# Decayed linear attention with 64 by 64 TensorE tiles, ahead of a snake feed-forward, on one core

## The chip, the core and the metric

One core of one Trainium2 chip. Its engines run their own instruction streams and meet through semaphores: TensorE (PE), VectorE (DVE), ScalarE (ACT), GpSimd (POOL), SyncE (SP), and 16 DMA engines that serve queues filled by SP and POOL. The metric is the device time of one execution in microseconds. The kernel before takes 219.55 us, the median of 5 runs (218.67 to 219.71).

## The reference

Attention with a decaying state, 4 sequences x 8 heads x 768 tokens x 64, then a feed-forward of 512 to 2048 to 512 over the 3072 tokens:

```python
gamma = 1.0 - 2.0 ** (-5.0 - np.arange(H))
for t in range(S):
    state = gamma * state + outer(k[t], v[t])        # per sequence and head
    y[t] = q[t] @ state / sqrt(D)
h = x @ w_in                                         # x: heads side by side
s = np.sin(alpha * h)
out = (h + s * s / alpha) @ w_out
```

## The kernel before

A sequence is cut in six chunks of 128 tokens, 24 chunks in all. The order P is: the four first chunks (e0 to e3), then the five others of sequence 0 (P4 to P8), of sequence 1 (P9 to P13), 2 (P14 to P18) and 3 (P19 to P23). Chunks go to the feed-forward in seven groups of 4, 2, 4, 4, 4, 4 and 2.

A chunk's attention is four steps on PE. *Scores*, `pa` (L213): per head K^T Q, 64 rows of the array by 128 columns. *Between chunks*, `py` (L247): the state times Q, with two heads' states in one block-diagonal 128 by 128 tile `s_bd`. *Mix*, `py` (L251): V times masked scores, 128 rows by 64 columns. *Sums*, `ps` (L227): K^T V added to the running state in PSUM. Each is eight matmuls, two of them side by side in the array. Around them DVE masks the scores into `aT` (L217) and scales `py` into `xT` (L258), and ACT copies `ps` to `s_bd` in two halves (L234). V is scaled by the decay beforehand (`scale_v`, L112), mostly on POOL. Q and K arrive with tokens on partitions and are turned either on PE (`stage_T`, with a copy by DVE or ACT) or by the DMA crossbar (`turn`, issued by SP, L205).

The feed-forward of a group runs in 16 slots of one 128-wide slice (8 double slots for the groups of 2): four matmuls into `ph` (L279), sine and square on ACT (L282, L287), `s * 1/alpha + ph` on DVE into `gT` (`Slot.add`, L294). Between the slots PE takes pieces of the second product of the group before (`ff_out`, `po`, L304), copied out by ACT (L316) and stored by SP.

All orders are written by hand: each engine executes what the program lists, in that order. Group 0 is interleaved by hand with the first attention chunks; `phase` runs the other groups and hangs attention steps on slots through the dictionary `att`. PSUM has eight banks: four rotate under the tag `mm` (`ph`, `po`, some `pt`), two hold `pa`, one each `ty` (`py`, `pt`) and `ps`.

POOL issues the loads, about 0.9 us for one. A load waits until the one eight before it on this queue has landed, and POOL's `scale_v` stand between the loads.

## Time and profile before

| | |
|---|---|
| median of 5 runs | 219.55 us |
| the profiled execution | 220.33 us |
| its span, first to last instruction | 218.6 us |
| PE, DVE, ACT, POOL busy | 207.2, 128.5, 162.7, 90.0 us |
| granted TensorE clock | 0.996 of full |

The profiled execution is 0.78 us over the median, and its own time is 1.8 us over its span. A row of the timeline is: start in us, length in us, engine, line, operation, output<-inputs, tile of the array, shapes, count, and in brackets how long the engine sat idle before and what ended that. Matmuls are pipelined, so lengths overlap; the distance between two starts is what a step costs.

### The profile page before, as it was taken

The page shows a single profiled execution, that of the slowest core. Times are in us where ns is not written, and L with a number is a line of the kernel's source. Part 1 is how long each engine was busy: PE and PEld are TensorE (multiplying, and loading weights), DVE is VectorE, ACT ScalarE, POOL GpSimd, SP SyncE. Part 2 cuts the span into 40 slices and gives each one's busy share as a digit, 9 for nine tenths or more (in the row PEclk, how much of TensorE's full clock was granted, in tenths as well). Part 3 has the DMA queues.
Part 4 walks back from the last instruction along what each step waited for, and adds up shares of the span by engine and source line. Part 5 has one row for each costly group of instructions (what it writes and reads, how often), then busy time and mean ns, then how long its engine had stood idle before and what let it go on. Part 6 is the DMA issues. An engine that isn't in the chain of part 4 may idle for free.

```text
span 218.6 us, 4245 instructions
## 1 busy us (share of the span) xinstructions
PE 207.2 (95%) x1661; PEld 107.4 (49%) x1661; DVE 128.5 (59%) x213; ACT 162.7 (74%) x311; POOL 90.0 (41%) x105
## 2 busy tenths in 40 slices
PE   7986899899999999999999999999999999999992
PEld 3443554457764544545455445455444544555540
DVE  4784849966896767766566556476464555233310
ACT  7776796668888999798778769768768876766610
POOL 8974434899859599293978100000000000000000
PEclk9999999999999999999999999999999999999998
DMA  9999999999999999999999946136111101111121
GB/s 132 147 190 189 206 207 165 149 192 169 163 138 176 116 154 154 113 117 165 136 183 144 78 96 76 39 82 75 25 49 51 48 0 51 48 48 48 51 93 51
DMA packets 99508, 24.67 MB, mean 113 GB/s; under 512 B 92304, under 2 KB 96416, under 8 KB 99488
## 3 DMA queue, kind: packets, MB, share of 16 engines
q0 software_dynamic: 77024, 13.37, 85.6%
q1 hardware_dynamic: 22464, 11.02, 25.9%
q8 instruction: 13, 0.21, 0.4%
q14 instruction: 7, 0.06, 0.1%
HBM read 27.27 MB, written 6.29 MB: 154 GB/s over the span
## 4 chain that ended last, share of the span: by engine, by line
PE 75%; DVE 10%; DMA 5%; POOL 4%; ACT 4%; issue 1%; POOLq 0%
PE po L304 36%; PE ph L279 31%; DMA qkr<-in_k_dram 5%; DVE gT L294 5%; PE py L247 3%; PE pa L213 2%; POOL qkr L83 2%; DVE aT L217 2%; PE py L251 2%; ACT s L282 1%; POOL vr L83 1%; DVE xT L258 1%; ACT s L287 1%; PE ps L227 1%; DVE s L289 1%
## 5 line engine op out<-in xcount | busy, mean ns | idle before, releaser
L294 DVE SCALAR_TENSOR_TENSOR gT<-s,rec_alpha,ph 128x512 bf16<-128x512 f32 (+3 forms) x120 | 74.2, 638 | 68.0 <-ACT s L287 67.4
L279 PE MATMUL ph<-xT,w_in 128*128 128x512 bf16 (+3 forms) x480 | 98.0, 337 | 1.3 <-DMA w_in<-in_moe_w_in_dram 0.5
L304 PE MATMUL po<-w_out,gT 128*128 128x512 bf16 x384 | 98.5, 380 | 0.6 <-DVE gT L294 0.6
L282 ACT ACTIVATE s<-ph,alpha_sb 128x512 f32<-128x512 f32 (+3 forms) x120 | 69.5, 601 | 35.6 <-PE ph L279 35.5
L279 PEld LDWEIGHTS <-w_in 128*128 128x128 bf16 x480 | 45.5, 98 | 42.9 <-issue 1.9
L287 ACT ACTIVATE s<-s 128x512 f32<-128x512 f32 (+1 forms) x94 | 58.4, 621 | 2.6
L304 PEld LDWEIGHTS <-gT 128*128 128x128 bf16 x384 | 35.2, 98 | 38.2 <-issue 0.6
L112 POOL TENSOR_TENSOR vr<-vr,kg 128x512 bf16<-128x512 bf16 x21 | 22.0, 1064 | 19.4 <-DMA vr<-in_v_dram 19.4
L217 DVE TENSOR_TENSOR aT<-pa,mask 128x1024 bf16<-128x1024 f32 x20 | 24.4, 1222 | 0.2 <-PE pa L213 0.2
L83 POOL DMA_DIRECT2D vr<-in_v_dram x24 | 21.8, 910 | 3.1 <-DMA w_in<-in_moe_w_in_dram 1.6
L83 POOL DMA_DIRECT2D qkr<-in_q_dram x23 | 21.3, 928 | 4.0 <-DMA w_out<-in_moe_w_out_dram 1.7
L83 POOL DMA_DIRECT2D qkr<-in_k_dram x23 | 20.6, 894 | 3.5 <-DMA w_out<-in_moe_w_out_dram 3.4
L234 ACT CAST s_bd<-ps 64x256 bf16<-64x256 f32 x40 | 14.4, 359 | 2.4 <-PE ps L227 2.1
L316 ACT COPY o_sb<-po 128x512 f32<-128x512 f32 x23 | 13.1, 575 | 4.0 <-PE po L304 3.9
L258 DVE TENSOR_TENSOR xT<-py,qg 128x512 bf16<-128x512 f32 x20 | 13.7, 685 | 2.7 <-PE py L251 2.7
L328 PE MATMUL spare<-warm 128*128 128x512 bf16 x28 | 9.5, 461 | 1.2 <-DVE warm L131 1.2
L213 PEld LDWEIGHTS <-qkT 64*128 64x128 bf16 x192 | 5.4, 94 | 9.3 <-issue 7.1
L251 PE MATMUL py<-aT,vr 128*64 128x128 bf16 x192 | 9.6, 220 | 0.4 <-DVE aT L217 0.4
L213 PE MATMUL pa<-qkT 64*128 64x128 bf16 x192 | 9.5, 219 | 0.4 <-ACT qkT L186 0.2
L247 PE MATMUL py<-qkT,s_bd 128*64 128x128 bf16 x160 | 8.3, 225 | 0.7 <-DVE xT L258 0.7
L247 PEld LDWEIGHTS <-s_bd 128*64 128x64 bf16 x160 | 5.4, 109 | 4.7 <-issue 2.0
L251 PEld LDWEIGHTS <-vr 128*64 128x64 bf16 x192 | 6.9, 110 | 1.3 <-issue 1.0
(59 smaller groups left out, 69.2 us busy)
## 6 DMA issues: line engine op xcount, KB each, us to landing
out_dram<-o_sb SPq DMA_DIRECT2D x24, 256.0 KB, 2.9
vr<-in_v_dram POOLq DMA_DIRECT2D x24, 128.0 KB, 6.5
qkr<-in_q_dram POOLq DMA_DIRECT2D x23, 128.0 KB, 5.6
qkr<-in_k_dram POOLq DMA_DIRECT2D x23, 128.0 KB, 6.0
w_in<-in_moe_w_in_dram POOLq DMA_DIRECT2D x4, 512.0 KB, 11.7
w_out<-in_moe_w_out_dram POOLq DMA_DIRECT2D x4, 512.0 KB, 15.9
q<-in_q_dram SPq DMA_DIRECT2D x1, 256.0 KB, 3.3
k<-in_k_dram SPq DMA_DIRECT2D x1, 256.0 KB, 4.1
```

Source lines behind the costliest of these rows:

```text
L83: nc.gpsimd.dma_start(out=t, in_=chunk_of(src, j))
L112: eng.tensor_mul(raw["v", j], raw["v", j], kg[:, j % NCH, :, None].to_broadcast([128, H, D]))
L213: nc.tensor.matmul(pa[:, e, p, :], qkT[r, NP + p, :], qkT[r, p, :], start=(p == 0), stop=True, skip_group_check=True)
L217: nc.vector.tensor_mul(aT.rearrange("p e n t -> p (e n) t"), pa.rearrange("p e n t -> p (e n) t"), m)
L247: nc.tensor.matmul(py[r, p, :], s_bd[c % 2][:, p, r], qkT[:, p, :], start=(p == 0), stop=True, skip_group_check=True)
L251: nc.tensor.matmul(py[64 * e:64 * e + 64, p, :], vs[:, 2 * p + e, :], aT[:, e, p, :], start=(c == 0 and p == 0), stop=True, skip_group_che ...
L258: nc.vector.tensor_mul(x, py, qg[:, c])
L279: nc.tensor.matmul(self.ph[:, m, :], w_in[:, i, f * 128:(f + 1) * 128], xT[g][:, i, self.lo:self.hi], start=(m == 0 and i == 0), stop=(i = ...
L282: nc.scalar.activation(out=self.s[:, m, :], in_=self.ph[:, m, :], func=ACTF.Sin, scale=alpha_sb[:, f:f + 1])
L287: nc.scalar.activation(out=self.s, in_=self.s, func=ACTF.Square)
L294: nc.vector.scalar_tensor_tensor(gT[self.g][:, f, self.lo:self.hi], self.s[:, m, :], rec_alpha[:, f:f + 1], self.ph[:, m, :], op0=ALU.mult ...
L304: nc.tensor.matmul(po[g, ts], gT[g][:, f, ts * C:(ts + 1) * C], w_out[:, f, :], start=(f == 0), stop=(f == FF - 1))
```

## The change

Every attention step after the first chunks takes 64 by 64 tiles where it can, four side by side: scores split each K tile in two halves of tokens (16 matmuls of 64x64 for 8 of 64x128), the step between chunks takes each head's 64 by 64 state alone (`inter`), without the block-diagonal copy. The heads' places in `xT` differ for half of the partitions, so `w_in` is loaded in three transfers instead of one. The state lives in SBUF (`s_f`, added to by DVE in `keep`) and is handed on in bf16 by one ACT copy (`hand_on`). The last sequence (`wide`) is loaded with 64 tokens per partition half, in 24 transfers (`load_seq`), its triangular halves are left out of scores and mix, its state is handed on by two POOL copies, and its `inter` is four full 128x128 matmuls. `pa` and `py` have two banks each, four are `mm`.

The steps are regrouped: a `burst` is `inter` and mix of one chunk with the scores of the next, so the mask has four slots before it is used. DVE's part of a burst is spread: mask in the slot, addition of the state and `xT` in the next; in group 1 mask and state come first, then the slot's `add`, then `xT`. P8 and P9 are turned on PE (copies on ACT), P10 and later by the crossbar, issued three chunks ahead. Later V are scaled by DVE, those of the last sequence by POOL. The last output tile leaves in three column pieces.

```diff
...
+    def wide(j):
+        return j % NCH > 0 and j // NCH == 3
+    def load_seq(bt):
+        nh = 2 * (NCH - 1)
+        tqk = big.tile([128, nh, 2, NP, D], BF16, name="qk_seq", tag="qk_seq", bufs=1)
+        tv = big.tile([128, nh, NP, D], BF16, name="v_seq", tag="v_seq", bufs=1)
+        for i, src in enumerate((q, k, v)):
+            for h in range(H):
+                r = slice(64 * (h // NP), 64 * (h // NP) + 64)
+                o = tv[r, :, h % NP, :] if i == 2 else tqk[r, :, i, h % NP, :]
+                nc.gpsimd.dma_start(out=o, in_=src[bt, h, C:, :].rearrange("(f i) d -> i f d", i=64))
+        for c in range(1, NCH):
+            j, f = bt * NCH + c, slice(2 * c - 2, 2 * c)
+            raw["qk", j], raw["k", j], raw["v", j] = tqk[:, f], tqk[:, f, 1], tv[:, f]
...
-        nc.gpsimd.dma_start(out=w_in[:, :, i * fw:(i + 1) * fw], in_=w_in_v[:, :, i * fw:(i + 1) * fw])
+        c = slice(i * fw, (i + 1) * fw)
+        nc.gpsimd.dma_start(out=w_in[:, 0:2, c], in_=w_in_v[:, 0:2, c])
+        for y in range(2):
+            nc.gpsimd.dma_start(out=w_in[64 * y:64 * y + 64, 2:4, c], in_=w_in_v[64 - 64 * y:128 - 64 * y, 2:4, c])
...
+    def later_tables():
+        for b in range(2):
+            r = slice(64 * b, 64 * b + 64)
+            for f in range(2):
+                nc.vector.tensor_scalar_add(tok[r, :, f], pos[r, :], float(64 * (f - b)))
+            nc.vector.tensor_copy(lgq[r], lg[r, NP * b:NP * b + NP])
+        for f in range(2):
+            nc.vector.tensor_mul(expoq[:, :, NP * f:NP * f + NP],
+                                 tok[:, :, f, None].to_broadcast([128, NCH, NP]),
+                                 lgq[:, None, :].to_broadcast([128, NCH, NP]))
+    def later_mask():
+        for t in s_w:
+            nc.vector.memset(t, 0.0)
+        for b in range(2):
+            nc.vector.tensor_scalar(maskq[64 * b:64 * b + 64, 0:128], tio[64 * b:64 * b + 64],
+                                    tok[64 * b:64 * b + 64, 0, 0:1], None, op0=ALU.is_ge)
...
+    s_f = big.tile([128, 2, 2, D], F32, name="s_f")
+    s_n = [big.tile([128, 2, 2, D], BF16, name=f"s_n{i}") for i in range(2)]
+    s_w = [big.tile([128, 2, 2, 128], BF16, name=f"s_w{i}") for i in range(2)]
...
+    tiles4 = [(b, e) for b in range(2) for e in range(2)]
...
+    def sums(j, py, base=256):
+        ks, vs = raw["k", j], raw["v", j]
+        for f in range(2 if wide(j) else 1):
+            for m in range(2):
+                for b, e in tiles4:
+                    o = py[half(e), b, base + 64 * m:base + 64 * m + 64]
+                    if not wide(j):
+                        h = 4 * b + 2 * m + e
+                        nc.tensor.matmul(o, ks[:, h, :], vs[:, h, :], start=(base == 0 and m == 0 and b == 0), stop=True,
+                                         skip_group_check=True)
+                    else:
+                        nc.tensor.matmul(o, ks[half(b), f, 2 * m + e, :], vs[half(b), f, 2 * m + e, :],
+                                         start=False, stop=True, skip_group_check=True)
+    def keep(j, py, base=256):
+        new = py[:, :, base:base + 128].rearrange("p b (m d) -> p m b d", m=2)
+        if j % NCH == 0:
+            nc.vector.tensor_copy(s_f, new)
+        else:
+            nc.vector.tensor_add(s_f, s_f, new)
+    def hand_on(j):
+        i = (j % NCH + 1) % 2
+        if not wide(j + 1):
+            nc.scalar.copy(s_n[i], s_f)
+            return
+        s = s_w[i].rearrange("p m b (y d) -> p m (b y) d", y=2)
+        nc.gpsimd.tensor_copy(s[half(0), :, 0:4:3], s_f[half(0)])
+        nc.gpsimd.tensor_copy(s[half(1), :, 1:3], s_f[half(1)])
+    def begin(j):
+        new = psum.tile([128, 2, 256], F32, name="new", tag="mm", bufs=4)
+        sums(j, new, 0)
+        keep(j, new, 0)
+    def inter(j):
+        new_py(j)
+        py, qkT, s = st["py", j], st["qkT", j], (s_w if wide(j) else s_n)[j % NCH % 2]
+        for m in range(2):
+            if wide(j):
+                for b in range(2):
+                    nc.tensor.matmul(py[:, b, m * 128:(m + 1) * 128].rearrange("p (f i) -> p f i", f=2),
+                                     s[:, m, b, :], qkT[:, m:m + 5:4, half(b)],
+                                     start=(m == 0), stop=True, skip_group_check=True)
+                continue
+            for b, e in tiles4:
+                nc.tensor.matmul(py[half(b ^ e), b, m * 128:(m + 1) * 128], s[half(e), m, b, :],
+                                 qkT[half(e), 2 * b + m, :], start=(m == 0), stop=True, skip_group_check=True)
+    def scores(j, tag="pa"):
+        qkT = st["qkT", j]
+        if not wide(j):
+            pa = psum.tile([128, 2, NP, 128], F32, name="pa", tag=tag)
             for p in range(NP):
-                for e in range(2):
-                    r = slice(64 * e, 64 * e + 64)
-                    nc.tensor.matmul(py[r, p, :], s_bd[c % 2][:, p, r], qkT[:, p, :],
-                                     start=(p == 0), stop=True, skip_group_check=True)
-        for p in range(NP):
-            for e in range(2):
-                nc.tensor.matmul(py[64 * e:64 * e + 64, p, :], vs[:, 2 * p + e, :], aT[:, e, p, :],
-                                 start=(c == 0 and p == 0), stop=True, skip_group_check=True)
...
-        if ps is not None:
-            keep_S(j, ps)
+                for f in range(2):
+                    for e in range(2):
+                        nc.tensor.matmul(pa[half(f), e, p, :], qkT[half(e), NP + p, half(f)], qkT[half(e), p, :],
+                                         start=(p == 0), stop=True, skip_group_check=True)
+            aT = work.tile([128, 2, NP, 128], BF16, name="aT0", tag="aT", bufs=2)
+            st["aT", j] = aT
+            return {"mask": lambda: nc.vector.tensor_mul(aT.rearrange("p e n t -> p (e n) t"),
+                                                         pa.rearrange("p e n t -> p (e n) t"), mask_bc)}
+        pa = psum.tile([128, 2, 512], F32, name="pa", tag="pa")
+        for m in range(2):
+            for b, e in tiles4:
+                nc.tensor.matmul(pa[half(b), e, 192 * m:192 * m + 128].rearrange("p (f i) -> p f i", f=2),
+                                 qkT[half(e), 2 + m, half(b)], qkT[half(e), m:m + 5:4, half(b)],
+                                 start=(m == 0), stop=True, skip_group_check=True)
+            for b, e in tiles4:
+                nc.tensor.matmul(pa[half(b), e, 192 * m + 128:192 * m + 192],
+                                 qkT[half(e), 6 + m, half(b)], qkT[half(e), 4 + m, half(b)],
+                                 start=False, stop=True, skip_group_check=True)
+        aT = work.tile([128, 2, 2, 192], BF16, name="aT", tag="aT", bufs=2)
+        st["aT", j] = aT
+        return {"mask": lambda: nc.vector.tensor_mul(aT, pa[:, :, 0:384].rearrange("p e (m t) -> p e m t", m=2),
+                                                     maskq[:, None, None, :].to_broadcast([128, 2, 2, 192]))}
+    def mix(j, first=None):
+        py, aT, vs, c = st["py", j], st["aT", j], raw["v", j], j % NCH
+        for m in range(2):
+            if not wide(j):
+                for b, e in tiles4:
+                    nc.tensor.matmul(py[half(b ^ e), b, m * 128:(m + 1) * 128], vs[:, 4 * b + 2 * m + e, :],
+                                     aT[:, e, 2 * b + m, :], start=False, stop=True, skip_group_check=True)
+                continue
+            for b, e in tiles4:
+                nc.tensor.matmul(py[half(b ^ e), b, m * 128:(m + 1) * 128], vs[half(b), 0, 2 * m + e, :],
+                                 aT[half(b), e, m, 0:128], start=False, stop=True, skip_group_check=True)
+            for b, e in tiles4:
+                nc.tensor.matmul(py[half(b ^ e), b, m * 128 + 64:(m + 1) * 128], vs[half(b), 1, 2 * m + e, :],
+                                 aT[half(b), e, m, 128:192], start=False, stop=True, skip_group_check=True)
+        now = j if c < NCH - 1 else first
+        if now is not None:
+            sums(now, py)
+        more = {"exit": lambda: nc.vector.tensor_mul(x_of(j), py[:, :, 0:256].rearrange("p b (m t) -> p b m t", m=2),
+                                                     qg[:, c].rearrange("p (b m) t -> p b m t", b=2))}
+        if now is not None:
+            more["keep"] = lambda: keep(now, py)
+            more["hand"] = lambda: hand_on(now)
+        return more
+    def burst(old, new, first=None):
+        inter(old)
+        return {**scores(new), **mix(old, first)}
+    def run(more, *kinds):
+        for kind in kinds or ("keep", "mask", "exit", "hand"):
+            if more and kind in more:
+                more.pop(kind)()
...
+    def last_tile(g, ts):
+        lo = 0
+        for n in (d_model // 2, d_model // 4, d_model // 4):
+            c = slice(lo, lo + n)
+            lo += n
+            ph = psum.tile([128, n], F32, name="poh", tag="mm", bufs=4)
+            for f in range(FF):
+                nc.tensor.matmul(ph, gT[g][:, f, ts * C:(ts + 1) * C], w_out[:, f, c],
+                                 start=(f == 0), stop=(f == FF - 1))
+            o_sb = work.tile([128, d_model], F32, name="o_sb", tag="o_sb", bufs=3)[:, :n]
+            if n > d_model // 4:
+                nc.scalar.copy(o_sb, ph)
+            else:
+                nc.vector.tensor_copy(o_sb, ph)
+            nc.sync.dma_start(out=out_view[:, groups[g][ts], c], in_=o_sb)
...
+    later_tables()
...
+    nc.scalar.activation(out=kgq, in_=expoq, func=ACTF.Exp, scale=-1.0)
...
+    def phase(g, outs, att, nf=1, calm=True, hold=0):
         no, done = len(outs), 0
         for n in range(FF // nf):
+            more, fresh = rest[0], {}
+            if not calm:
+                run(more, "hand")
             now = Slot(g, n * nf, nf=nf).sq("A")
+            run(more, "keep", "exit", "hand")
             for fn in att.get(n, ()):
-                fn()
-            now.add()
-            while done < no * (n + 1) * nf // FF:
+                fresh.update(fn() or {})
+            if calm:
+                run(fresh, "mask")
+                now.add()
+            else:
+                run(fresh, *(("keep", "exit") if n == FF // nf - 1 else ("mask", "keep")))
+                now.add()
+                run(fresh, "exit", "mask")
+            if fresh:
+                assert not more
+                rest[0] = fresh
+            while done < ((no - hold) * (n + 1) * nf // FF if n < FF // nf - 1 else no):
...
-    po[0, 0] = psum.tile([128, d_model], F32, name="po", tag="ps")
-    po[0, 1] = psum.tile([128, d_model], F32, name="po", tag="ty")
+    pair = psum.tile([128, 2, d_model], F32, name="po", tag="pa")
+    po[0, 0], po[0, 1] = pair[:, 0, :], pair[:, 1, :]
     F((0,), range(4))
     F((1,), range(3))
     b.add()
+    for j in (e0, e1, e2, e3):
+        scale_v(j, nc.vector)
     a = Slot(0, 0, (n3, n4), 4)
     F((1,), (3,))
...
     a = Slot(0, 13)
+    begin(e0)
     b.sq("D").add()
     F((0, 1), (9,))
     b = Slot(0, 14)
+    hand_on(e0)
     a.sq("A").add()
...
     a = Slot(0, 15)
     b.sq("D").add()
+    scale_v(P[4], nc.vector)
     a.sq("A").add()
     F((0, 1), (11, 12))
-    stage_A(P[4])
-    scale_v(P[4], nc.vector)
+    run(scores(P[4], "py"))
+    scale_v(P[5], nc.vector)
     F((0, 1), (13, 14))
-    stage_T(P[5], nc.scalar, "mm")
-    F((0, 1), (15,))
+    stage_T(P[5], nc.scalar)
+    ff_out(0, 0, 15, False)
+    ff_out(0, 1, 15, False)
+    tile_out(0, 0)
+    tile_out(0, 1)
...
     scale_v(P[8], nc.gpsimd)
-    scale_v(e1, nc.gpsimd)
-    for n in range(11, NJ + 2):
-        scale_v(P[n - 2], nc.gpsimd)
-        if n < NJ:
-            load_chunk(P[n])
-        if n in (13, 15):
-            scale_v(P[(n - 9) // 2], nc.gpsimd)
+    load_chunk(P[11])
+    scale_v(P[9], nc.gpsimd)
+    load_chunk(P[12])
+    load_chunk(P[13])
+    for j in P[14:19]:
+        load_chunk(j)
+    load_seq(3)
...
     fill(3)
-    stage_A(P[5])
-    SK(e0)()
-    scale_v(P[5], nc.vector)
+    stage_T(P[6])
+    run(burst(P[4], P[5]), "keep", "hand", "mask", "exit")
+    fill(4)
+    stage_T(P[7], nc.scalar)
     fill(5)
-    stage_M(P[4])
-    fill(4)
-    stage_M(P[5])
+    more = burst(P[5], P[6])
+    run(more, "exit", "keep")
+    stage_T(P[8], nc.scalar)
+    run(more, "hand", "mask")
     fill(4)
     phase(1, outs,
-          {0: [T(P[6]), X(P[8])], 1: [A(P[6])], 2: [T(P[7]), X(P[9])], 3: [A(P[7]), M(P[6])], 4: [X(P[10])],
-           5: [A(P[8]), M(P[7])], 6: [X(P[11]), A(P[9]), M(P[8]), SK(e1)], 7: [M(P[9])]}, 2)
+          {0: [T(P[9])], 1: [B(P[6], P[7]), X(P[10])], 3: [B(P[7], P[8]), X(P[11])],
+           5: [B(P[8], P[9], e1)], 6: [X(P[12])], 7: [B(P[9], P[10])]}, 2, calm=False, hold=6)
+    att = {}
+    def at(n, fn):
+        att.setdefault(max(n, 0), []).append(fn)
+    at(11, later_mask)
+    n, base = 10, 0
+    for g in range(2, NG - 1):
+        count = FF if sizes[g] > 2 else FF // 2
+        for i, j in enumerate(groups[g + 1]):
+            a = base + (i + 1) * count // len(groups[g + 1]) - 3
+            new = P[n + 1] if n + 1 < NJ else None
+            at(a - (4 if wide(j) else 2), V(j))
+            if n + 3 < NJ:
+                at(a - 2, X(P[n + 3]))
+            if new is not None:
+                at(a, B(j, new, new - 1 if new % NCH == 1 else None))
+            else:
+                at(a - 1, I(j))
+                at(a, M(j))
+            n += 1
+        base += count
+    base = 0
     for g in range(2, NG):
-        att = {}
-        if g + 1 < NG:
-            js = groups[g + 1]
-            for i, j in enumerate(js):
-                a = i * FF // len(js) + 1
-                n = P.index(j) + 2
-                if n < NJ:
-                    att.setdefault(a + 1, []).append(X(P[n]))
-                att.setdefault(a, []).append(A(j))
-                if i > 0:
-                    att[a].append(M(js[i - 1]))
-                if j % NCH == 1:
-                    att[a].append(SK(j - 1))
-            att.setdefault(FF - 2, []).append(M(js[-1]))
-        phase(g, out_pieces(g - 1, range(sizes[g - 1])), att, 1 if sizes[g] > 2 else 2)
-    for fn in out_pieces(NG - 1, range(sizes[-1])):
+        count = FF if sizes[g] > 2 else FF // 2
+        phase(g, out_pieces(g - 1, range(sizes[g - 1])), {s - base: fns for s, fns in att.items()},
+              FF // count)
+        base += count
+    for fn in out_pieces(NG - 1, range(sizes[-1] - 1)):
         fn()
+    last_tile(NG - 1, sizes[-1] - 1)
...
```

## The prediction

> **What bounds the kernel now.** I read the page first: PE is busy in nearly every slice, and the DMA engines are full until about 125 us.
>
> ```profile
> PE 207.2 (95%) x1661; PEld 107.4 (49%) x1661; DVE 128.5 (59%) x213; ACT 162.7 (74%) x311; POOL 90.0 (41%) x105
> ...
> PE   7986899899999999999999999999999999999992
> ...
> DMA  9999999999999999999999946136111101111121
> ```
>
> Then PE's waits after the start; they say where PE is not the bound.
>
> ```profile
> PE pt L195 <- DMA qkr<-in_q_dram: 1.9, 1, 1.9
> PE py L247 <- DVE xT L258: 0.7, 3, 0.3
> ...
> PE pt L195 <- DMA qkr<-in_k_dram: 0.4, 1, 0.4
> ```
>
> So up to about 40 us loads pace PE, around 62 to 66 us (end of group 1) DVE's `xT`, and from 66.1 us on PE alone. The sum over the rest checks that: from 92.1 to the last matmul at 214.25, 48 slots of 1.73 us, eight double slots of 2.60 and 32 final matmuls of 0.216 make 110.7 us, and ten chunks of attention at 1.11 make 11.1; 121.8 of 122.1.
>
> Third, PE's timeline at one chunk in the steady part. The reader is to take the distances between starts.
>
> ```profile
> 101.27 1.03 PE L279 MATMUL ph<-xT,w_in 128*128 128x512 bf16 x4
> 102.23 0.40 PE L213 MATMUL pa<-qkT 64*128 64x128 bf16 x8
> 102.55 0.41 PE L247 MATMUL py<-qkT,s_bd 128*64 128x128 bf16 x8
> 102.80 0.39 PE L251 MATMUL py<-aT,vr 128*64 128x128 bf16 x8
> 103.02 0.29 PE L227 MATMUL ps<-vr,qkr 128*64 128x64 bf16 x8
> 103.25 1.04 PE L304 MATMUL po<-w_out,gT 128*128 128x512 bf16 x4
> ```
>
> `ph` streams until 102.13 (four times 0.216), so a chunk costs 1.11 us. In single instructions each pair of matmuls starts 3 to 4 ns apart and the next pair 55 ns later (31 ns in `ps`): pairs already share the array. Three times the tile shape changes (into `pa`, into `py`, back to `po`), each with about 0.09 us of empty stream.
>
> Fourth, DVE at the end of group 1, where it has no gaps.
>
> ```profile
> 60.30 1.22 DVE L217 TENSOR_TENSOR aT<-pa,mask 128x1024 bf16<-128x1024 f32 x1
> 61.43 0.68 DVE L258 TENSOR_TENSOR xT<-py,qg 128x512 bf16<-128x512 f32 x1
> 62.03 0.86 DVE L294 SCALAR_TENSOR_TENSOR gT<-s,rec_alpha,ph 128x256 bf16<-128x256 f32 x2
> 62.81 1.22 DVE L217 TENSOR_TENSOR aT<-pa,mask 128x1024 bf16<-128x1024 f32 x1
> ```
>
> Start to start: mask 1.13, `xT` 0.60, a double slot's two adds 0.78.
>
> **The change part by part, quads on PE.** No row shows four 64x64 tiles at once. Bounds: four take one pair's 55 ns, or two pairs' 111 ns. I take 55: pairs split by rows (L213) and pairs split by columns (L247) both overlap in full. For P4 to P17 `inter` falls from 0.22 to 0.11, scores stay at 0.22 (16 matmuls in quads), mix 0.22 and sums 0.125 stay, three shape changes stay: 1.11 becomes about 0.985. A wide chunk: `inter` 0.22 as four full matmuls that need no shape change, scores and mix 0.17 each, sums 0.125, two changes: 0.88. At 111 ns per quad they cost 1.32 and 1.35.
>
> A rule that speaks against this: the Trainium skill, TensorEngine Tiling (Array Packing), Gotcha 1: PSUM Pressure, says "Different row tiles cannot access same PSUM bank simultaneously". In `inter` of the narrow chunks both row halves write bank b at once, on different partitions; in the rows, L247 has two column tiles in one bank at full speed, but no two row tiles. If the rule meant serial execution, `inter` would stay at 0.22 and the time would be about 219.4 by it.
>
> **Start, to 38.7 us.** `later_tables` puts eight tiny DVE operations ahead of the first `aT`; tiny ones take 0.06 (memset) to 0.62 us (`rec_alpha`), so 0.8 to 2.8 us together. That delays the first feed-forward by at most about a microsecond, and behind it PE waits 1.94 us for e3's Q at 20.0; `early(4)` (0.65 us of PE) also moves into that wait. Costed at zero; without the cover up to 1.5. `w_in` in three pieces adds eight POOL issues of about 0.8 us. The queue is seven transfers deep there, and e3's Q, issued 2.8 us later, still stands behind 5 us of transfers: zero, bounds 0 to 1.5. The four `scale_v` of e0 to e3 (0.69 each, 2.8) fall in a DVE gap of 2.6 us before the adds at 29.4. `begin` (0.3 PE, 0.35 DVE) and the earlier `scale_v` of P4 fall before PE's stop for P4's K at 38.7, which a DMA sets.
>
> **38.7 to the end of group 1.** Here I count a loss. P8 and P9 now need PE (0.45 each); that saves two crossbar transfers. With the turns of P6, P7 and P8 ahead of group 1, PE comes to the K of P6 (landed 44.0: issue 36.9 plus 7.1) and from there takes P6's turn, a burst, four `po`, P7's turn, five `po`, a burst, P8's turn and four `po`: 0.4 + 1.05 + 0.86 + 0.45 + 1.08 + 1.05 + 0.45 + 0.86 = 6.2 us, to slot 0 at 50.2. At 51.1 it wants to turn P9, whose K is still coming:
>
> ```profile
> L83 POOL DMA_DIRECT2D qkr<-in_k_dram x1: 893/893/893, 46.7 to 46.7; - x1
> ...
> DMA to landing us min/median/max: 5.9/5.9/6.0
> ```
>
> 46.7 + 6.0 = 52.7, a new stop of about 1.5 us (before, P9 was turned by the crossbar and needed at 61.6). Nothing in the diff moves that load: POOL's scaling of P6 still stands ahead of it.
>
> Then seven double slots and four bursts. PE alone would need 7 x 0.865 + 8 x 0.216 + 4 x 1.0 + 1.73 (the eight last pieces) = 13.5 us, so group 2 from 66.4. But DVE and ACT turn in a loop per burst: state addition in `keep` (0.35, near the 0.39 that one 256-wide add takes of the 0.78; bounds 0.30 and 0.48, that add's full length), handed on by ACT before the next sines (0.40; the half copies of L234 take 0.36), sines and square 0.84 + 0.63, adds 0.78, mask 1.13: 4.1 us, against 3.3 of PE for two double slots with a burst. `inter` waits for `py` until `xT` is out. Laid end to end from 52.9, bursts begin at 54.0, 57.5, 61.6 and 65.75, and group 2 begins when the last `xT` (68.0) and the held pieces (68.5) are done: 68.5, against 66.1 before: **+2.4**. Bounds: +0.5 (loop hidden, P9 earlier) to +4.5 (each burst another half microsecond). The crossbar for P10 can go at about 56 and took 5 to 8 us before; it is needed at 65.8: no cost.
>
> **Group 2.** Before: 26.0 us = 16 x 1.30 + 4 x 1.11 + waits of 0.4 (`xT`), 0.35 (ACT's `o_sb`) and rounding. After: 20.75 + 3.94, as the deferred `xT` and `py`'s own banks take both waits away. **-1.3**. DVE has 4 adds of 0.66, mask, `xT`, `keep` and 0.69 of `scale_v` per four slots, 5.4 of 6.2 us; `later_mask` (about 1.2) comes on top once, within the three slots that four `mm` banks allow.
>
> **From group 3 on.** Ten chunks of attention before, 4.45 + 4.45 + 2.2 = 11.1; after 3.94 + (0.92 + 3 x 0.88) + (0.88 + 0.22 + 0.35) = 8.95. **-2.2**. Hidden: ACT has one copy of 0.40 for two of 0.36; POOL's two state copies (0.5 to 1.1 each by the 1.06 of its 128x512 multiply) have four slots, 7 us; `load_seq` costs POOL 24 issues for 15, 21 us, and is in by about 97 while the crossbar wants it at 110. If this cover failed, each late chunk would stop PE visibly.
>
> **The end.** Before, the last matmul at 214.25 is followed by two copies in series (0.42, 0.37) and a store.
>
> ```profile
> 214.45 0.42 DVE L313 COPY o_sb<-po 128x256 f32<-128x256 f32 x1 [6.23 <-PE po L304]
> 214.91 0.37 ACT L314 COPY o_sb<-po 128x256 f32<-128x256 f32 x1 [3.33 <-DVE o_sb L313]
> 215.31 0.33 SPq L317 DMA_DIRECT2D out_dram<-o_sb  x1
> ```
>
> After, one copy of 128 columns (0.29, between L313's 0.42 and a tiny one's 0.16) ends it, and 48 short matmuls cost 0.1 more than 16 long ones: **-0.4**.
>
> Sum: +2.4 - 1.3 - 2.2 - 0.4 = -1.5. The profiled 220.33 becomes 218.8; that execution is 0.78 over the median, so against runs 219.55 - 1.5 = **218.05**.
>
> **Rivals.**
> - *Group 1 loses nothing.* For it: DVE is near its limit there already, and PE's own sum is 66.4. Against: ACT's copy before the sines. The +2.4 becomes about +0.4: 216.0.
> - *Row tiles wait for a bank in `inter`*: 15 bursts at 0.11, less what group 1 hides, +1.3: 219.4.
> - *DVE's loop in group 1 is slower than laid out* (the side slower than before): bursts of 4.8 us and a late P9 begin group 2 at 71.2, +5.1 in place of +2.4: 220.75. For it: DVE ran without gaps at 60 to 66, and four operations of the loop have no row of their own. It decides against the change once group 2 begins later than 70.0.
> - *Quads run as two pairs*: bursts 0.34 dearer than I took (narrow) and 0.47 (wide), about +6 over my sum: 224. Against it: both pair rows overlap in full.
>
> **How the numbers follow.** Sum as laid out 0.42; nothing lost in group 1 0.17; bank 0.10; slow loop 0.20; pairs 0.11. My own case spans 217.0 to 219.0. The range 215.5 to 221.4 leaves out the pairs and a little at each end. Within 0.3% (218.9 to 220.2) is what this kernel's measurement cannot tell from no change: most of the bank case and the edges of two others, 0.15. Faster: most of the first and all of the second, 0.55. Slower: the slow loop, the pairs, 0.30.
>
> **What would show it.** Right: narrow bursts of 0.98 and wide of 0.88 us from `ph` to `po`; quads 55 ns apart; PE waiting about 1.5 us for P9's K near 51; group 2 beginning near 68.5; no PE gaps after 70; the last copy near 0.3. Wrong: quads 111 ns apart, a group 2 beginning before 66.5 or after 70, waits for a crossbar or for POOL's state copies.

## The result, and the profile after

The changed kernel takes 220.19 us (median of 21 runs, 219.37 to 220.60); the kernel before took 219.30 in the same comparison (40 runs). The ratio is 1.0042, 95% interval 1.0030 to 1.0054: 0.9 us slower, where 1.5 us faster was forecast. Both profiled executions lie above the medians of their kernels, at 220.54 and 220.33 us, and their spans differ by only 0.17 us (218.74 against 218.56). Why the medians differ by more is part of the explanation.

The page after shows PE still at 94% and DVE at 65% (59% before) with 257 instructions (213 before):

```profile
PE 205.6 (94%) x1921; PEld 108.6 (50%) x1921; DVE 142.3 (65%) x257; ACT 157.1 (72%) x289; POOL 90.0 (41%) x120
...
DMA  9999999999999999999993340310011011111112
```

PE's own waits from 38 us on, after the change. The columns are the tile and line, what it waited for, total us, times, longest:

```profile
PE py L354 <- DVE xT L405: 2.0, 3, 0.9
PE py L354 <- ACT s_n L331: 0.4, 1, 0.4
PE ph L441 <- ACT o_sb L472: 0.4, 1, 0.4
PE pt L256 <- DMA qkr<-in_k_dram: 0.4, 1, 0.4
...
PE ph L441 <- DVE xT L405: 0.3, 1, 0.3
```

The first is the loop of group 1, the fourth the stop for P9's K. The three waits for `xT` in PE's timeline:

```profile
57.71 0.31 PE L354 MATMUL py<-qkT,s_n 64*64 64x128 bf16 x8 [0.38 <-DVE xT L405]
...
61.92 0.31 PE L354 MATMUL py<-qkT,s_n 64*64 64x128 bf16 x8 [0.71 <-DVE xT L405]
...
66.13 0.31 PE L354 MATMUL py<-qkT,s_n 64*64 64x128 bf16 x8 [0.93 <-DVE xT L405]
```

DVE and ACT wait for each other there. First DVE's adds, which wait for ACT's square, then ACT's state copy, which waits for DVE's addition and stands ahead of the next sines:

```profile
58.05 0.87 DVE L456 SCALAR_TENSOR_TENSOR gT<-s,rec_alpha,ph 128x256 bf16<-128x256 f32 x2 [0.49 <-ACT s L449]
...
60.42 0.41 ACT L331 CAST s_n<-s_f 128x256 bf16<-128x256 f32 x1 [1.01 <-DVE s_f L325]
```

The second, third and fifth wait all lie in group 2, which the forecast had without a wait. The same three in PE's timeline:

```profile
71.56 0.31 PE L354 MATMUL py<-qkT,s_n 64*64 64x128 bf16 x8 [0.44 <-ACT s_n L331]
...
83.63 1.02 PE L441 MATMUL ph<-xT,w_in 128*128 128x512 bf16 x4 [0.43 <-ACT o_sb L472]
...
95.27 1.02 PE L441 MATMUL ph<-xT,w_in 128*128 128x512 bf16 x4 [0.35 <-DVE xT L405]
```

The bracket counts from PE's last modelled end. From start to start, the stream lacks 0.61, 0.60 and 0.51 us at these places. Before the change the second one cost 0.35 us:

```profile
79.66 1.02 PE L279 MATMUL ph<-xT,w_in 128*128 128x512 bf16 x4 [0.18 <-ACT o_sb L316]
```

ACT around the second one, after the change:

```profile
80.21 0.69 ACT L444 ACTIVATE s<-ph,alpha_sb 128x512 f32<-128x512 f32 x1 [0.84 <-PE ph L441]
80.93 0.63 ACT L449 ACTIVATE s<-s 128x512 f32<-128x512 f32 x1
81.47 0.39 ACT L331 CAST s_n<-s_f 128x256 bf16<-128x256 f32 x1
81.76 0.68 ACT L444 ACTIVATE s<-ph,alpha_sb 128x512 f32<-128x512 f32 x1
82.47 0.63 ACT L449 ACTIVATE s<-s 128x512 f32<-128x512 f32 x1
83.01 0.57 ACT L472 COPY o_sb<-po 128x512 f32<-128x512 f32 x1
```

ACT runs six operations without a gap, so the copy that frees the bank starts when PE already wants it.

PE at one narrow burst after, to be held against the chunk shown before (1.11 us there):

```profile
104.93 1.03 PE L441 MATMUL ph<-xT,w_in 128*128 128x512 bf16 x4
105.89 0.31 PE L354 MATMUL py<-qkT,s_n 64*64 64x128 bf16 x8
106.02 0.39 PE L365 MATMUL pa<-qkT 64*64 64x128 bf16 x16
106.35 0.41 PE L392 MATMUL py<-aT,vr 128*64 128x128 bf16 x8
106.59 0.29 PE L313 MATMUL py<-vr,qkr 128*64 128x64 bf16 x8
106.82 1.04 PE L465 MATMUL po<-w_out,gT 128*128 128x512 bf16 x4
```

`ph` streams until 105.80, so a burst costs 1.02 us (0.985 forecast). In single instructions the four 64x64 matmuls of a quad start within 10 ns, and in the scores the next quad starts 55 ns later, as a pair did before: quads share the array in full.

The end after, and the stretches of the two profiled executions:

```profile
213.80 0.37 ACT L487 COPY o_sb<-poh 128x256 f32<-128x256 f32 x1 [1.16 <-PE poh L483]
214.20 2.10 SPq L490 DMA_DIRECT2D out_dram<-o_sb  x3
214.75 0.29 DVE L489 COPY o_sb<-poh 128x128 f32<-128x128 f32 x1 [5.47 <-PE poh L483]
215.64 0.29 DVE L489 COPY o_sb<-poh 128x128 f32<-128x128 f32 x1 [0.60 <-PE poh L483]
```

| stretch | before | after | difference | forecast |
|---|---|---|---|---|
| start to P4's scores | 41.16 | 40.98 | -0.2 | 0 |
| to group 2's first `ph` | 24.94 | 27.82 | +2.9 | +2.4 |
| to group 3's first `ph` | 25.85 | 26.47 | +0.6 | -1.3 |
| to the end of the last matmul | 122.30 | 120.11 | -2.2 | -2.2 |
| to the end of the span | 4.31 | 3.36 | -1.0 | -0.4 |

(The forecast took group 2's end at 92.1, where the last `po` of the first slot of group 3 runs; its first `ph` is at 91.95.)

### The profile page after: what moved, and what is told of

Same layout as the page of the kernel before. It is cut to its first block, busy times and chain, and to the rows that moved or that the text cites. A ratio compares the mean times of both kernels' runs of the same rounds, so it can differ in the third digit from the quotient of the medians.

```text
span 218.7 us, 4771 instructions
## 1 busy us (share of the span) xinstructions
PE 205.6 (94%) x1921; PEld 108.6 (50%) x1921; DVE 142.3 (65%) x257; ACT 157.1 (72%) x289; POOL 90.0 (41%) x120
## 4 chain that ended last, share of the span: by engine, by line
PE 63%; DMA 18%; DVE 6%; POOL 5%; ACT 4%; issue 2%; POOLq 0%; DVEq 0%
PE po L465 30%; PE ph L441 26%; DMA w_in<-in_moe_w_in_dram 7%; DMA w_out<-in_moe_w_out_dram 5%; DMA vr<-in_v_dram 3%; DMA qkr<-in_k_dram 3%; POOL qkr L89 2%; DVE gT L456 2%; ACT s L444 2%; POOL vr L89 2%; PE poh L483 2%; DVE aT L369 2%; ACT s L449 1%; PE py L392 1%; PE py L354 1%
## 5 line engine op out<-in xcount | busy, mean ns | idle before, releaser
L444 ACT ACTIVATE s<-ph,alpha_sb 128x512 f32<-128x512 f32 (+3 forms) x120 | 69.5, 600 | 37.7 <-PE ph L441 36.3
L89 POOL DMA_DIRECT2D vr<-in_v_dram x19 | 17.2, 903 | 5.0 <-DMA qkr<-in_q_dram 2.7
L369 DVE TENSOR_TENSOR aT<-pa,mask 128x1024 bf16<-128x1024 f32 x15 | 18.3, 1221 | 1.1 <-PE pa L365 0.7
L89 POOL DMA_DIRECT2D qkr<-in_q_dram x18 | 16.4, 912 | 2.9 <-DMA w_out<-in_moe_w_out_dram 1.2
L142 DVE TENSOR_TENSOR vr<-vr,kg 128x512 bf16<-128x512 bf16 x15 | 10.0, 685 | 0.0
L104 POOL DMA_DIRECT2D qk_seq<-in_q_dram x8 | 5.7, 714 | 8.9 <-DMA qkr<-in_k_dram 4.5
L331 ACT CAST s_n<-s_f 128x256 bf16<-128x256 f32 x15 | 5.9, 395 | 4.1 <-DVE s_f L325 3.0
L258 ACT COPY qkT<-pt 128x1024 bf16<-128x1024 bf16 x5 | 5.0, 1010 | 3.4 <-PE pt L256 3.4
L142 POOL TENSOR_TENSOR v_seq<-v_seq,kgq 128x512 bf16<-128x512 bf16 x5 | 5.2, 1040 | 5.5 <-ACT s L449 5.2
L325 DVE TENSOR_TENSOR s_f<-s_f,py 128x256 f32<-128x256 f32 x16 | 6.6, 415 | 0.5 <-PE py L313 0.5
L354 PE MATMUL py<-qkT,s_n 64*64 64x128 bf16 x120 | 4.6, 227 | 2.5 <-DVE xT L405 2.0
```

What stands on the lines that cost most here:

```text
L89: nc.gpsimd.dma_start(out=t, in_=chunk_of(src, j))
L142: eng.tensor_mul(t, t, by[:, j % NCH, :, None].to_broadcast([128, H, D]))
L354: nc.tensor.matmul(py[half(b ^ e), b, m * 128:(m + 1) * 128], s[half(e), m, b, :], qkT[half(e), 2 * b + m, :], start=(m == 0), stop=True, ...
L369: return {"mask": lambda: nc.vector.tensor_mul(aT.rearrange("p e n t -> p (e n) t"), pa.rearrange("p e n t -> p (e n) t"), mask_bc)}
L444: nc.scalar.activation(out=self.s[:, m, :], in_=self.ph[:, m, :], func=ACTF.Sin, scale=alpha_sb[:, f:f + 1])
```

## The experiments

**Both kernels once more.** Nothing is edited.

> The kernel before once more, unchanged, for a second profiled execution: the first one (220.33) was 1.0 above the median of that kernel's runs, and the two profiles compared so far differ by 0.1 us where the medians differ by 0.9. Theory (that execution lost its microsecond at its start or at its end, where DMA decides): the last matmul of this one comes earlier by up to 1 us, all of it before 45 us; from the last ph of group 0 on the two agree within 0.2 us. Rival (the steady part varies as well): they differ in groups 1 to 3.

> The changed kernel once more, unchanged, on the chip of the two runs beside it. Theory (PE's stop for P9's K, which lands at 52 to 53.3 whatever PE does, sets its time): the profile shows P4's scores somewhere in 40.2 to 41.2 and P9's K turned at 52.2 to 53.2; from the first burst of group 1 to the last matmul 160.9 to 161.3 us. About 220.2 to 220.7, 0.4% over the kernel before.

Before: 219.27 us; after: 220.17, ratio 1.0033 (1.0009 to 1.0057). The two new profiles agree at P4's scores. First the kernel before, then the changed one:

```profile
40.34 0.40 PE L213 MATMUL pa<-qkT 64*128 64x128 bf16 x8
...
65.28 1.02 PE L279 MATMUL ph<-xT,w_in 128*128 128x512 bf16 x4
```

```profile
40.30 0.42 PE L365 MATMUL pa<-qkT 64*64 64x128 bf16 x16
...
51.41 0.40 PE L256 MATMUL pt<-ident,qkr 128*128 128x128 bf16 x4 [0.59 <-DMA qkr<-in_q_dram]
52.27 0.40 PE L256 MATMUL pt<-ident,qkr 128*128 128x128 bf16 x4 [0.46 <-DMA qkr<-in_k_dram]
...
68.43 0.81 PE L441 MATMUL ph<-xT,w_in 128*128 128x512 bf16 x3
```

The kernel before starts 0.82 us earlier than in its first profile and ends 0.84 earlier (span 217.72 against 218.56): from P4's scores on, 177.4 us in both, so between these two only its start varies. The changed kernel starts 0.68 earlier than in its first profile, but its stop for P9 grows from 1.07 to 1.39 us and it gains only 0.36 at group 2. An early start is partly eaten by P9's K, which lands only 0.36 us earlier (52.22 against 52.58). In this pair group 1 costs +3.2, group 2 +0.3 (its last stop is 0.21 here and in most executions, 0.51 in the first), the rest -2.2 and the end -0.9. That is +0.4 in all, so it does not account for the whole 0.9 between the medians. Six profiled executions, these two included, have the program of the changed kernel up to group 2. P4's scores to group 2 takes 27.82 to 28.58 us in them, 28.25 in the mean, and the first profile is the lowest.

**Group 1: P9's turn in a later slot.**

```diff
-          {0: [T(P[9])], 1: [B(P[6], P[7]), X(P[10])], 3: ...
+          {1: [B(P[6], P[7]), X(P[10])], 2: [T(P[9])], 3: ...
```

> The changed kernel with one edit: P9 is turned on PE in slot 2 of group 1 instead of slot 0. Theory (P9's K, landed at 52.58, stops PE for 1.2 us, and that moves everything behind it): PE does not stop there, the first burst of group 1 begins near 52.6 instead of 54.04, group 2 near 67.5, time about 219.0. Rival (the loop of DVE and ACT paces the rest of group 1 anyway, and ACT's copy of 1.0 us now stands in it): the bursts come closer at first and are held by xT later; group 2 begins no more than 0.4 us earlier; 219.8 to 220.2.

219.26 us, 0.9992 of the kernel before (0.9967 to 1.0017): the loss is gone. PE's timeline of it is below. PE does not stop at 52; from P4's scores to group 2 it takes 27.03 us, against 28.13 above. But a new stop of 0.87 us stands ahead of the second burst (56.50): `ph` waits until DVE's adds have freed a bank, and these stand behind the mask and the state addition. ACT's copy of P9, which the rival names, is not its cause, as it begins only when that stop is over. That the new `pt` takes a bank which `ph` now lacks is argued: in the crossbar run below, which has no `pt` at this place, the stop is missing.

```profile
51.81 0.31 PE L354 MATMUL py<-qkT,s_n 64*64 64x128 bf16 x8
...
55.53 1.03 PE L441 MATMUL ph<-xT,w_in 128*128 128x256 bf16 x8 [0.87 <-DVE gT L456]
56.50 0.31 PE L354 MATMUL py<-qkT,s_n 64*64 64x128 bf16 x8
```

```profile
54.62 0.86 DVE L456 SCALAR_TENSOR_TENSOR gT<-s,rec_alpha,ph 128x256 bf16<-128x256 f32 x2
...
56.44 0.99 ACT L258 COPY qkT<-pt 128x1024 bf16<-128x1024 bf16 x1
```

**P9 by the crossbar again**, in slot 0 (`{0: [X(P[9])], ...`).

> The changed kernel with one edit: P9 is turned by the crossbar (as in the kernel before), issued in slot 0 of group 1, instead of on PE. Theory (the turn on PE costs group 1 its stop of 1.2 us for P9's K, 0.43 us of PE and 1.0 us of ACT): no stop near 52, first burst of group 1 near 52.4, P9 lands near 60 and is wanted at about 60.5; group 2 begins near 67.5 and the time is about 218.8 to 219.3, a little below the run with the turn moved to slot 2 (219.26). Rival (the crossbar lands after the third burst of group 1 wants it, or DVE's 3.7 us of work a burst paces group 1 in any case): scores of the third burst wait for a DMA, or xT waits grow by what was saved; 219.6 or more.

219.21 us, 0.9982 (0.9959 to 1.0005). P9 landed at 59.66 and nothing waited for it. But the waits for `xT` went from 2.0 to 2.8 us: what PE saved, DVE's loop took back in part, and the result is that of the later turn.

**w_in in one transfer a part**, so POOL has eight issues less; run twice.

```diff
-        nc.gpsimd.dma_start(out=w_in[:, 0:2, c], in_=w_in_v[:, 0:2, c])
-        for y in range(2):
-            nc.gpsimd.dma_start(out=w_in[64 * y:64 * y + 64, 2:4, c], ...)
+        nc.gpsimd.dma_start(out=w_in[:, :, c], in_=w_in_v[:, :, c])
```

> The changed kernel with w_in loaded as before, one transfer for each of its four parts instead of three. Its rows of heads 4 to 7 then don't stand where the new order of heads wants them, so the feed-forward's values are not the reference's; the work is the same. Theory (eight POOL issues of about 0.8 us less ahead of e3's Q and K bring those earlier, and PE waits for e3's K at 19 to 20.5 us): e3's K arrives up to 1 us earlier, everything behind moves with it, about 219.6 against 220.1. Rival (as the prediction had it, the transfers ahead in the queue set the time and not the issues): no change, 220.1.

> The changed kernel with w_in loaded in one transfer a part, as before (values not the reference's), a second time, for its size on one chip with the changed kernel and for a second profile. Theory (P9's K comes earlier by what POOL saves): PE turns P9's K before 52.0 in this profile, and the time is 0.8 to 1.5 us below the changed kernel's on this chip. Rival (the first result was an accident of that chip): less than 0.4 us below.

> The two edits together: w_in in one transfer a part (values not the reference's), and P9 turned in slot 2 of group 1. Alone, the turn in slot 2 stood at 0.9992 of the kernel before and w_in at 0.997. Theory (w_in's pieces act through P9's K): with the turn out of the way w_in brings nothing more, 0.997 to 0.999 of the kernel before. Rival (they act at the start, through e3's K or P4's): the gains add, 0.992 to 0.994.

First time 219.25, 0.9970 (0.9949 to 0.9991); second time 219.50, 1.0012 (0.9987 to 1.0036), 0.67 below the changed kernel on the same chip. The second profile has P4's scores at 40.30, as the changed kernel's above, so the two can be read side by side:

```profile
50.74 0.40 PE L254 MATMUL pt<-ident,qkr 128*128 128x128 bf16 x4
51.32 0.40 PE L254 MATMUL pt<-ident,qkr 128*128 128x128 bf16 x4 [0.18 <-DMA qkr<-in_k_dram]
```

P9's K is there 0.95 us earlier and the last matmul comes 0.94 earlier (213.72 against 214.66). The profile of the first run does not repeat this:

```profile
52.27 0.40 PE L254 MATMUL pt<-ident,qkr 128*128 128x128 bf16 x4 [0.33 <-DMA qkr<-in_k_dram]
```

There P9's K is turned at the same 52.27 as in the changed kernel above, and only the stretch from P4's scores to group 2 is shorter, 27.22 us, because P4's scores come late, at 41.21. With one transfer a part P9's K landed at 51.28, 51.82 and 52.22 us, with three pieces at 52.04 to 53.28 in twelve profiled executions. The first theory, an earlier e3's K, fell: that K was turned at 20.37 and 19.39, not earlier than in the changed kernel (19.1 to 20.3 in its executions). With both edits 219.13, 0.9991 (0.9967 to 1.0015), the same as the turn alone (0.9992). So the extra issues cost time, and as far as intervals of half a microsecond can tell they cost it through P9's K and not otherwise. How much is less certain, as the two runs' ratios lie 0.4% apart.

**DVE's order in group 1.**

```diff
-                run(fresh, *(("keep", "exit") if n == FF // nf - 1 else ("mask", "keep")))
+                run(fresh, "keep", "exit")
```

> The changed kernel with one edit: in group 1 DVE does the state addition and xT of a burst first, then the adds, and the mask last (now: mask, addition, adds, xT). Theory (group 1 is late because xT, which frees py for the next burst, stands behind 2.5 us of other DVE work): the waits of inter for xT at 57.71, 61.92 and 66.13 (0.55, 0.88, 1.09 beyond the stream) shrink together by 0.9 or more, the bursts come 3.6 to 3.8 us apart instead of 3.67, 4.21 and 4.21, group 2 begins near 67.8, and the time is about 219.2 to 219.5. Rival (DVE's amount of work, not its order, paces group 1; the state copy on ACT holds the sines): bursts stay 4.1 to 4.2 apart and the time near 220.2.

219.88 us, 1.0026 (1.0011 to 1.0041). Only a third of the theory held: from the first burst (54.04 in both) group 2 begins 14.42 us later instead of 14.76. No burst waits for `xT`; the scores wait for the mask instead, and DVE's timeline is nearly without gaps:

```profile
57.94 0.86 DVE L456 SCALAR_TENSOR_TENSOR gT<-s,rec_alpha,ph 128x256 bf16<-128x256 f32 x2
59.00 0.42 DVE L325 TENSOR_TENSOR s_f<-s_f,py 128x256 f32<-128x256 f32 x1 [0.20 <-PE py L313]
59.34 0.68 DVE L405 TENSOR_TENSOR xT<-py,qg 128x512 bf16<-128x512 f32 x1
59.94 0.86 DVE L456 SCALAR_TENSOR_TENSOR gT<-s,rec_alpha,ph 128x256 bf16<-128x256 f32 x2
60.72 1.22 DVE L369 TENSOR_TENSOR aT<-pa,mask 128x1024 bf16<-128x1024 f32 x1
```

State additions come 3.92 us apart, and the idle time left is 0.2.

**State additions left out in slots 1, 3 and 7** (`fresh.pop("keep", None)` there).

> The changed kernel with DVE's state additions of slots 1, 3 and 7 of group 1 (0.33 to 0.35 us each) left out, so that the states of batches 0 and 1 miss three chunks; everything else, ACT's copy of the state too, is as it was. Theory (DVE's amount of work sets the distance of the bursts in group 1): the waits for xT at 57.71 and 61.92 shrink by 0.35 each, group 2 begins about 1.0 us earlier than at 68.80, 219.2. Rival (the loop is ACT's copy, sines and squares, and DVE only follows): bursts stay 4.2 apart and the time near 220.2.

219.09 us, 0.9990 (0.9973 to 1.0007). The states lack three additions, so the values are not the reference's. From first burst to group 2 13.75 us in place of 14.76: 1.0, three times 0.34. So the loop runs through the state addition. That DVE's amount of work alone sets it is not shown: without the addition ACT's state copies don't wait for it either (0.56 and 1.01 us in the changed kernel), and DVE still stands idle for 0.58 us once.

**Group 2's first stop: P9's state handed on earlier** (`run(rest[0], "hand")` behind group 1's phase).

> The changed kernel with one edit: P9's state is handed on (ACT's copy into s_n) before group 2's first slot instead of behind that slot's sine and square. Theory (the first new stop of group 2 is an order of ACT's queue): PE's stop of 0.61 us before P10's `inter` at 71.56 goes, the stops at 83.63 (0.60) and 95.27 (0.51) stay, so group 3 begins about 0.6 us earlier than at 95.27 and the time is about 0.5 to 0.6 below the changed kernel's 220.19: 219.6. Rival (DVE paces group 2, 5.4 us of work in 6.2 plus `later_mask`): the stop goes and comes back at the next bank wait or at group 3's start; group 3 still begins near 95.2 and the time stays near 220.2.

219.67 us, 1.0018 (0.9998 to 1.0038). In its trace P10's `inter` starts without a wait, and nothing takes the wait's place: group 3's first `ph` follows group 2's after 25.66 us (26.47 and 26.17 in the changed kernel). ACT's timeline: the state copy now stands ahead of the sine.

```profile
69.85 0.41 ACT L331 CAST s_n<-s_f 128x256 bf16<-128x256 f32 x1
70.23 0.69 ACT L444 ACTIVATE s<-ph,alpha_sb 128x512 f32<-128x512 f32 x1
```

**Group 2's third stop: the mask later** (`at(11, later_mask)` becomes `at(22, later_mask)`).

> The changed kernel with one edit: `later_mask` (two memsets of 0.55, two comparisons of 0.75 on halves, a small copy: 1.3 us of DVE from 89.15 to 90.49) is done in slot 6 of group 3 instead of slot 11 of group 2. Theory (it makes DVE late with the last xT of group 2): PE's stop of 0.51 us at group 3's first ph goes; about 219.7. Rival (scale_v of P13 at 90.49 and P13's mask are enough to make DVE late; or the slot 22 has no room either): the stop stays, or another appears near slot 6 of group 3; about 220.2.

219.94 us, 1.0032 (1.0015 to 1.0049): no gain that can be measured. The stop at group 3's first `ph` goes, and 1.9 us later PE waits 0.17 for the output copy. As most profiled executions have 0.21 there, not the 0.51 of the first profile, there was little to win.

**Group 2's second stop: the state copy behind the output copy** (in slots 6 and 7 of group 2 `run(more, "hand")` is skipped, so it runs in slot 8).

> The changed kernel with one edit: in group 2 the state of slot 6 is handed on (ACT's copy into s_n, 0.39 us) in slot 8 instead of slot 6, behind the copy of po that PE waits for at 83.63. Theory (that state copy pushes ACT's copy of po back by 0.3 us): the copy of po starts 0.2 us earlier, as soon as po is done, the stop shrinks from 0.60 to 0.40, about the 0.35 of before, and nothing else changes: 220.0. Rival (the bank is late for another reason, or inter of slot 9 now waits for s_n): the stop stays 0.60, or one of 0.3 or more appears at 84.6.

220.75 us, 1.0047 (1.0031 to 1.0063). The stop shrinks from 0.60 to 0.35, the value of the kernel before; `inter` of slot 9 now stops 0.69 us for `s_n`, since the copy runs only at 84.56, behind slot 8's sine and square. So 0.25 of this stop is the state copy's, and the place to avoid it isn't there.

**A bank of its own for `po`.**

```diff
...
-            po[g, ts] = psum.tile([128, d_model], F32, name="po", tag="mm", bufs=4)
+            if g < NG - 1:
+                po[g, ts] = psum.tile([128, d_model], F32, name="po", tag="po")
+            else:
+                po[g, ts] = psum.tile([128, d_model], F32, name="po", tag="mm", bufs=3)
...
```

(three banks for the rest)

> The changed kernel with one edit: the output accumulator po has a bank of its own and ph, pt and the rest have three (now: four shared by all; group 0's slots 3, 7, 11 and 15 use po's bank). Theory (PE's stop of 0.60 us at 83.63 comes because the next ph takes the bank that po just held, so it waits for ACT's copy of 0.57): the next ph takes another bank, the next po has a whole ph of 0.86 us until it needs its own, and the stop goes; later in group 2 and at group 3's start nothing new: about 219.6. Rival (three banks for ph are too few where DVE's adds are late, or the loss comes back at group 3's start, where DVE is the late one): stops before ph for gT appear, 220.2 or more.

228.37 us, 1.0400 (1.0350 to 1.0451). The next `po` waits for its own copy 13 times, and bursts in group 3 come 8.29 us apart for 7.94. The theory forgot that ACT's copy stands behind the slot's sine and square, so a `ph` is no cover for it. Three banks also cost time ahead of group 2, where `ph` waits 3.3 us for `gT` (0.9 in the changed kernel). PE's wait for the output copy, in the same columns as above:

```profile
PE po L470 <- ACT o_sb L477: 3.6, 13, 0.9
```

**The old end** (one accumulator, two half copies, one store, as before).

> The changed kernel with its end undone: the last tile is one accumulator of 16 long matmuls, copied half by DVE and half by ACT and stored in one transfer, as before. By the prediction's term (-0.4 for the new end) it becomes 0.4 slower: 220.6. By what the two profiles show from the last long matmul on (last matmul to end 4.3 us before and 3.3 after, for 0.1 us more of PE) it becomes 0.9 to 1.0 slower: 221.1. Rival (three stores cost what the shorter copy saves): 220.2, no change.

220.84 us, 1.0057 (1.0033 to 1.0081). The medians give +0.65, the ratios +0.3, with the start varying in both. The trace is plainer: from the end of the last matmul to the end of the span 4.40 us, against 3.36 and 3.39 after and 4.31 and 4.28 before.

**The order of the tiles in `inter`.**

```diff
...
+        if not wide(j):
+            for b, e in tiles4:
+                for m in range(2):
+                    nc.tensor.matmul(...)
+            return
         for m in range(2):
...
```

> The changed kernel with one edit: in `inter` of the narrow chunks the two matmuls of one 64x64 tile are issued one after the other (tile A twice, then B, C, D), instead of the four tiles in turn, twice. Theory (four tiles run side by side, PE issues in order, and a tile is busy 55 ns with 128 columns): A's second waits for its first, and B's first starts with it, so five steps of 55 ns take the place of two: inter 0.17 us longer, 15 times less what group 1 hides, about 1.5 to 2.0 us slower than 220.19: 222. Rival (the row halves of one bank are written in turn anyway, or the matmuls are reordered): no change, 220.2.

220.02 us, 1.0034 (1.0018 to 1.0049): no change. `inter` takes 0.136 us as before. Its eight starts still come as four and four. Within a four they are 7 ns apart where it was 3, but so they are in this run's scores, which have no edit.

**Four edits together, with a fifth**: the state of P9 handed on early, the mask later, DVE's new order, P9 turned in slot 2. The run has one edit more, which its expectation does not name: the copy of an output tile is held back until the next slot's matmuls have been listed.

```diff
...
+            leave_due()
             for m, f in enumerate(self.fs):
...
-            tile_out(g, ts)
+            due.append((g, ts))
...
```

> The changed kernel with four edits together: P9's state handed on before group 2's first slot, `later_mask` in slot 6 of group 3, state addition and xT first and the mask last in group 1, P9 turned in slot 2 of group 1. Alone they gave 219.67, 219.94, 219.88 and 219.26 where the changed kernel has 220.19. If they act on separate waits, their gains add: 0.52 + 0.25 + 0.31 + 0.93 = 2.0, so 218.2, about 0.9 below the kernel before (219.15). Rival (DVE's total work from 50 to 95 us is the bound, and each edit only moves its queue): less than 1.2 of it, 219.0 or more, with new waits for DVE in group 2.

217.48 us, 0.9901 of the kernel before (0.9866 to 0.9937): 1.4% below the changed kernel by the ratios, more than the separate gains (2.0 us) promised. P4's scores to group 2 26.24 us, group 2 25.45 (25.85 before the change). Group 2 holds just the separate gains of the early state and the later mask (0.51 and 0.21 off the 26.17 of the second profile). The surplus lies in group 1: from first burst to group 2 14.71 us, where the turn alone has 15.50 and the new order alone took 0.33 off. The fifth edit has no run of its own. Against the run below, which lacks it, ACT's order differs by it in one place alone, an output copy that moves behind P9's state copy (66.07) to 67.44. That is after the last burst of group 1 (63.87), so the surplus isn't its work; that the turn and the new order help each other is likely, and not shown. What PE still waits for from 38 us on:

```profile
...
PE pa L365 <- DVE aT L369: 0.8, 2, 0.5
PE ph L441 <- DVE gT L457: 0.7, 2, 0.4
PE ph L441 <- ACT o_sb L478: 0.4, 1, 0.4
```

> As the run with four edits together (217.48), but P9 is turned by the crossbar in slot 0 of group 1 instead of on PE in slot 2. Theory (with the new order DVE has a tenth of a microsecond to spare per burst, so what PE and ACT save, 0.43 and 1.0 us, shows): the stop of 0.50 before the second burst goes, group 2 begins about 0.5 us earlier than at 67.24, 217.0. Rival (DVE's amount of work per burst is what is left): group 2 begins at the same time, 217.4 to 217.6.

This run differs from the one above in two things, not one as its expectation has it: P9 goes by the crossbar, and output copies are not held back. It was not better: 219.21 us, 0.9970 (0.9946 to 0.9994), with single runs from 217.67 to 222.21. The profile is of the run at 222.21 us, far from the median, and no stretch is read from it. Why it gives back part of what the run above wins stays open.

## Why the prediction was wrong

**The step that failed first is group 2, "take both waits away. -1.3".** The stretch came out 0.3 to 0.6 us longer. PE's work fell as counted, but three stops stand where two were written off: 0.61, 0.60 and 0.21 to 0.51 us, which is the whole way from the 24.7 us forecast to the 26.17 and 26.47 measured. (1) P9's state is added in the last slot of group 1, while `hand` runs in group 2 behind a sine and a square; P10's `inter` waits 0.61. The forecast priced ACT's copy by its length, hidden from group 3 on as "one copy of 0.40 for two of 0.36", and never asked when it runs; handing on earlier removed the stop. (2) `o_sb` was said to go with `py`'s own banks, but the bank was `mm`'s, not `py`'s. It grew from 0.35 to 0.60, and moving the state copy showed those 0.25 to be that copy's. (3) DVE's 5.4 of 6.2 us was right as a mean and no bound at one place: `xT` comes 0.2 late (0.5 once) at group 3's start. The "three slots that four `mm` banks allow" cover adds, not an `xT` that the next group needs at once.

**Group 1: the mechanisms were right, +2.4 was too small.** Bursts were laid out at 54.0, 57.5, 61.6 and 65.75 and came at 54.04, 57.71, 61.92 and 66.13, `xT` late each time. The loop through addition, state copy, sines, adds and mask was laid out at 4.1 us and came at 4.21. Leaving out additions showed that it runs through them, and the new order that 0.3 us could be had without that. The stop for P9's K was put at 1.5 us and was 1.07 and 1.39 in the two profiles, and up to 1.85 in runs with the same program up to there. What the sum lacks is that this stop is measured against a moving start. The row it was read from belongs to an execution whose start was 0.8 us late. The kernel before passes an early start on to its end in full. P9's K passes on about half: it landed at 52.73 and 52.34 us in the two profiles of the kernel before, which start 0.82 us apart, and at 52.58 and 52.22 in those of the changed kernel, 0.68 apart. In the executions that agree at P4's scores the step is +3.2, and over six executions +3.3. So the first two profiles differ by less than the medians: that of the kernel before is 1.0 us above its median by its late start, that of the changed kernel only 0.35, with the shortest group 1 of the six. The stretches account for 0.4 to 0.5 of the 0.9 us; where the rest lies the runs don't show.

**w_in's issues: "zero, bounds 0 to 1.5".** They cost 0.67 us by the medians on one chip, and by the ratios 0.5 the second time and 1.6 the first, so zero was too low and the bounds about right. The working looked at e3's Q alone, whose cover did hold; it failed to follow the same eight issues down POOL's queue to P9's K. "Nothing in the diff moves that load" came true as far as the load goes: 52.7 us was forecast and 52.58 measured. What it missed is that the load would come earlier without the eight issues, at 51.28 to 52.22. Why it then comes earlier than in the kernel before, with as many POOL instructions ahead of it, stays open.

**The end: -0.4 was mis-sized,** -0.9 to -1.0 from the last matmul on. The forecast counted the shorter copies; the last store, 64 KB for 256, also lands in 1.57 us instead of 2.03.

**Right:** the start from loads to the first `ph`; quads at 55 ns; narrow bursts of 1.02 (0.985); wide ones 0.105 cheaper, as counted (their slots repeat after 7.84 us for 7.94); group 3 on -2.2; no stop for a crossbar transfer, for POOL's state copies or for `load_seq` (in by 115 us, not the 97 forecast, still in time). The rivals of pairs and of the bank fell with the quads. What the Trainium skill's TensorEngine Tiling (Array Packing) says in Gotcha 1: PSUM Pressure, that different row tiles cannot access one bank at the same time, this trace does not bear out as a price: in `inter` both row halves write bank b and start 3 ns apart. The "slow loop" rival had the sign but not the mechanism: it wanted bursts 4.8 us apart and group 2 to begin after 70.0 us; they came 4.21 apart, and it began at 68.4 to 69.5.

## What to carry to other kernels

A wait is written off only with the name of the buffer it was for and with the place of the instruction that frees it in its engine's queue: a copy that costs nothing by its length can hold PE for 0.6 us by its place. A stop for a transfer has no fixed price: here it ate about half of what an early start gained, so its price has to be taken over several executions, not from the profiled one. And an engine at nine tenths of a stretch can be the bound wherever its work comes in a row; move work to it only where there is slack at that place.

## What the runs showed of the hardware

Two 64x64 matmuls of one tile, issued one after the other, do not hold up those of the other tiles behind them: eight issued as A, A, B, B, C, C, D, D still start as four and four 80 ns apart (the first step holds a change of tile shape; 55 ns later in the scores). How PE gets past the waiting one the trace does not say, as it doesn't name the tile.

One and the same DVE comparison on 64x128 took 0.45 us in one execution and 0.15 in another, and by the same 0.30 us group 3's stop differs between them, 0.51 against 0.21: a short stop read from one execution can be more than half chance.
